# First block of a transformer layer: transposed copies of tiles 0 and 1 in quarters, tiles 2 and 3 transposed by DMA from ScalarE's queue

## The chip, the cores and the metric

The kernel runs on one core of a Trainium2 chip. The metric is the device time of one execution in microseconds; a lower number is better. Five engines work side by side, each through its own instruction stream in order: TensorE (matmul, PE in the profile, with its weight loads as PEld), VectorE (DVE), ScalarE (ACT), GpSimd (POOL) and SyncE (SP), which only issues DMAs here. ScalarE can issue DMAs too; such an instruction stands in its stream among the others.

## The reference

One layer with pre-normalization, on x of 2048 rows and 1024 columns in bfloat16: sliding-window attention with 32 heads and a window of 256, then a dense block with SiLU.

```python
def _layernorm(x, axis=-1, eps=1e-5):
    m = jnp.mean(x, axis=axis, keepdims=True)
    v = jnp.var(x, axis=axis, keepdims=True)
    return (x - m) / jnp.sqrt(v + eps)

def _A_ref(x, wqkv, wo):
    B, S, D = x.shape
    H = 32; Dh = D // H; W = 256
    qkv = (lambda x, *d: x.transpose(*d))((x @ wqkv).reshape(B, S, 3, H, Dh), 2, 0, 3, 1, 4)
    q, k, v = qkv[0], qkv[1], qkv[2]
    scores = jnp.einsum("bhqd,bhkd->bhqk", q, k) * (Dh ** -0.5)
    idx = jnp.arange(S)
    mask = (idx[:, None] - idx[None, :] >= 0) & (idx[:, None] - idx[None, :] < W)
    scores = jnp.where(mask[None, None], scores, -1e9)
    p = _softmax(scores, axis=-1)
    o = jnp.einsum("bhqk,bhkd->bhqd", p, v)
    return (lambda x, *d: x.transpose(*d))(o, 0, 2, 1, 3).reshape(B, S, D) @ wo

def _B_ref(x, w1, w2):
    h = _silu(jnp.einsum("bsd,df->bsf", x, w1))
    return jnp.einsum("bsf,fd->bsd", h, w2)

h = x + _A_ref(_layernorm(x, axis=-1), A_wqkv, A_wo)
h2 = h + _B_ref(_layernorm(h, axis=-1), B_w1, B_w2)
```

## The kernel before

The 2048 rows are worked on in four blocks of 512 rows, and a block in four tiles of 128 rows. The order of the instructions on every engine is written out by hand; waits on semaphores are put in where one engine needs another's result. The change touches the start of block 0 only.

For TensorE the normalized rows must lie transposed, with the 1024 model columns on the partitions in eight pieces of 128 (called kt). `lnT_b[0]` holds them for block 0. For each tile j the way there is: a load of x (`load_x`, L139), statistics on VectorE (`ln_half` L170, then L178), a square root on ScalarE (L206), a reciprocal on VectorE (L209), the normalization on VectorE in two halves of 512 columns (`ln_norm`, L198), and the transpose. The transpose is done in one of two ways. `turn_first` does it on TensorE: four transposes of 128x128 (L217) into one PSUM bank, then one copy of 512 columns by ScalarE into `lnT_b` (L218), for each of two halves. `ln_transpose` does it with one DMA (L202), from SBUF to SBUF, issued from SP's queue. In the kernel before, tiles 0, 1 and 2 of block 0 go through `turn_first`, and tile 3 through `ln_transpose`. The two PSUM banks for the transposes are those that later hold the attention output (`o_ps`, under the name `tp_ps`).

When tile 0 is there, TensorE begins with the V products (`v_group`, L239): for tile j and half c of wv's columns, eight matmuls of 512 columns add up in one of two accumulator banks (`acc`), and ScalarE casts the sum into `v` (L241). The order of the groups (j, c) is (0,0), (1,0), (0,1), (1,1), (2,0), (2,1), (3,0), (3,1). The transposes of tile 1 stand inside the first group, half by half ahead of its matmuls 5 and 7; those of tile 2 stand after the third group. After the V products come the q and k products of the block (`qk_group`, L249), 128 matmuls, and then the attention scores, in the banks `sc`, beside the V, q and k products of block 1.

SP's queue loads in this order: x tile 0, the first half of wv, its second half, x tiles 2 and 3, and the first of four parts of the q/k weights, of 1 MB each (`load_wqkv`, L143). x tile 1 is loaded from ScalarE's queue. Then SP issues tile 3's transpose, and only after it the other three parts of the q/k weights and the x tiles of block 1. Eleven matmuls on zeros (L166) run on TensorE before the first data arrives.

Of the kernel before, what the change touches and what calls it, by code (L numbers as in the profile page):

```python
# [8 lines left out]
BF16 = mybir.dt.bfloat16  # L9
F32 = mybir.dt.float32  # L10
# [4 lines left out]
P = 128  # L15
# [33 lines left out]
def kernel(  # L49
# [10 lines left out]
    nc = tc.nc  # L60
# [3 lines left out]
    S, D = x2d.shape  # L64
# [25 lines left out]
    r_e = big.tile([P, 12288], BF16, name="r_e")  # L90
    r_n = big.tile([P, 1536], BF16, name="r_n")

    ps_sc = tc.tile_pool(name="ps_sc", bufs=1, space=bass.MemoryType.PSUM, reuse_waits="tile")
    sc_pool = ps_sc.__enter__()
    sc = [sc_pool.tile([P, 2, 512], F32, name=f"sc{i}") for i in range(2)]
    o_ps = [ps.tile([P, 8, 64], F32, name=f"o_ps{i}") for i in range(2)]
    tp_ps = [t[:].rearrange("p a b -> p (a b)").bitcast(BF16) for t in o_ps]
    acc_ps = [ps.tile([P, 512], F32, name=f"acc{i}") for i in range(2)]

    def view(region, off, *dims):  # L100
        n = 1
        for d in dims:
            n *= d
        ap = region[:, off:off + n]
        if len(dims) == 2:
            return ap.rearrange("p (a b) -> p a b", b=dims[1])
        if len(dims) == 3:
            return ap.rearrange("p (a b c) -> p a b c", b=dims[1], c=dims[2])
        return ap
# [4 lines left out]
    lnT_b = [view(r_w, 24576, KT, 512), view(r_t, 0, KT, 512)]  # L114
    x_ring = [view(r_o, i * 1024, 1024) for i in range(8)]
# [22 lines left out]
    def load_x(b, j, queue=nc.sync):  # L138
        queue.dma_start(out=x_ring[(b % 2) * 4 + j], in_=x2d[(b * 4 + j) * P:(b * 4 + j + 1) * P, :])  # L139

    def load_wqkv(c0):
        dst = wqk[:, :, c0:c0 + 512] if c0 < 2 * D else wv[:, :, c0 - 2 * D:c0 - 2 * D + 512]
        nc.sync.dma_start(out=dst, in_=wqkv_v[:, :, c0:c0 + 512])  # L143
# [6 lines left out]
    load_x(0, 0)  # L150
    load_wqkv(2 * D)
    load_x(0, 1, nc.scalar)
    load_wqkv(2 * D + 512)
    load_x(0, 2)
    load_x(0, 3)
    load_wqkv(0)

    ident = const.tile([P, P], BF16, name="ident")
    make_identity(nc, ident[:])
    warm = ebuf[0]  # L160
# [2 lines left out]


    for i in range(11):
        nc.tensor.matmul(sc[0][:, i % 2, :], lhsT=warm[:, 0, 0:P], rhs=warm[:, 0, :], start=True, stop=True)  # L166


    def ln_half(xt, stats, c):
        nc.vector.bn_stats(out=stats[:, c, :], in_=xt[:, c * 512:(c + 1) * 512])  # L170

    def ln_stats(xt, st, j, half_done=None):
        stats = half_done
        if stats is None:
            stats = small.tile([P, 2, 6], F32, name="ln_st", tag="ln_st")
            ln_half(xt, stats, 0)
        ln_half(xt, stats, 1)
        nc.vector.bn_aggr(out=st[:, j, :], in_=stats[:])  # L178
# [18 lines left out]
    def ln_norm(xt, st, rs, j):  # L197
        nc.vector.tensor_scalar(out=xt, in0=xt, scalar1=st[:, j, 0:1], scalar2=rs[:, j:j + 1],  # L198
                                op0=ALU.subtract, op1=ALU.mult)

    def ln_transpose(xt, dst, j):
        nc.sync.dma_start_transpose(out=dst[:, :, j * P:(j + 1) * P], in_=xt)  # L202

    def ln_first(xt, st, rs, j, half_done=None, ahead=None):
        ln_stats(xt, st, j, half_done)
        nc.scalar.activation(out=rs[:, j:j + 1], in_=st[:, j, 1:2], func=ACT.Sqrt, bias=eps[:], scale=1.0)  # L206
        if ahead is not None:
            ln_half(ahead[0], ahead[1], 0)
        nc.vector.reciprocal(out=rs[:, j:j + 1], in_=rs[:, j:j + 1])  # L209
        for h in range(2):  # L210
            ln_norm(xt[:, h * 512:(h + 1) * 512], st, rs, j)

    def turn_first(xt, dst, j, halves=(0, 1)):
        for h in halves:
            for i in range(4):
                kt = h * 4 + i
                nc.tensor.transpose(out=tp_ps[h][:, i * P:(i + 1) * P], in_=xt[:, kt * P:(kt + 1) * P], identity=ident[:])  # L217
            nc.scalar.copy(out=dst[:, h * 4:(h + 1) * 4, j * P:(j + 1) * P],  # L218
                           in_=tp_ps[h][:, 0:512].rearrange("p (k q) -> p k q", q=P))

    def ln_tiles(tag):
        st = small.tile([P, 4, 2], F32, name=f"st_{tag}", tag=f"st_{tag}")
        rs = small.tile([P, 4], F32, name=f"rs_{tag}", tag=f"rs_{tag}")
        return st, rs
# [5 lines left out]
    def next_acc():  # L230
        acc_n[0] += 1
        return acc_banks[acc_n[0] % len(acc_banks)]

    def v_group(b, j, c, copy, between=None):
        acc = next_acc()
        for kt in range(KT):
            if between:
                between(kt)
            nc.tensor.matmul(acc, lhsT=lnT_b[b % 2][:, kt, j * P:(j + 1) * P], rhs=wv[:, kt, c * 512:(c + 1) * 512],  # L239
                             start=(kt == 0), stop=(kt == KT - 1))  # L240
        copy(out=v[:, b * 4 + j, c * 16:(c + 1) * 16, 0:DH], in_=acc.rearrange("p (h d) -> p h d", d=DH))  # L241
# [146 lines left out]
    st, rs = ln_tiles("a")  # L388
    half = small.tile([P, 2, 6], F32, name="ln_st", tag="ln_st")
    ln_first(x_ring[0], st, rs, 0, None, (x_ring[1], half))  # L390
    turn_first(x_ring[0], lnT_b[0], 0)
    ln_first(x_ring[1], st, rs, 1, half)

    def turn_1(kt):
        if kt in (5, 7):
            turn_first(x_ring[1], lnT_b[0], 1, (kt // 2 - 2,))

    v_group(0, 0, 0, act, turn_1)
    ln_first(x_ring[2], st, rs, 2)
    v_group(0, 1, 0, act)  # L400
    v_group(0, 0, 1, act)
    turn_first(x_ring[2], lnT_b[0], 2)
    ln_first(x_ring[3], st, rs, 3)
    ln_transpose(x_ring[3], lnT_b[0], 3)
    for c0 in (D, 512, D + 512):
        load_wqkv(c0)
    v_group(0, 1, 1, act)
    v_group(0, 2, 0, act)
    v_group(0, 2, 1, act)
    nc.scalar.activation(out=dummy[:], in_=eps[:], func=ACT.Exp)  # L410
    v_group(0, 3, 0, act)
    v_group(0, 3, 1, act)
    for j in range(4):
        load_x(1, j)

    def ln1_steps(b):
        st, rs = ln_tiles("a")
        xs = [x_ring[(b % 2) * 4 + j] for j in range(4)]
        steps = [lambda j=j: ln_stats(xs[j], st, j) for j in range(4)]
        steps += rstd_steps(st, rs)  # L420
        for j in range(4):
            steps.append(lambda j=j: ln_norm(xs[j], st, rs, j))
        return steps, [lambda j=j: ln_transpose(xs[j], lnT_b[b % 2], j) for j in range(4)]

    def ln2_steps(b):
        st, rs = ln_tiles("b")
        hb = h_blk[b]
        load = lambda: nc.sync.dma_start(out=hb, in_=h_dram[b * 512:(b + 1) * 512, :].rearrange("(j p) d -> p j d", p=P))
        steps = [load]
        steps += [lambda j=j: ln_stats(hb[:, j, :], st, j) for j in range(4)]  # L430
        steps += rstd_steps(st, rs)
        for j in range(4):
            steps.append(lambda j=j: ln_norm(hb[:, j, :], st, rs, j))
        turns = [lambda j=j: ln_transpose(hb[:, j, :], ln2T[b], j) for j in range(4)]
        return steps[:-2] + [turns[0], steps[-2], turns[1], steps[-1]] + turns[2:]
# [22 lines left out]
    def between(kt):  # L458
        k, m = count
        if m * len(first_bursts) >= k * 192:  # L460
            run_late()
            scores_first(k)
            if pending:
                pending.pop(0)()
            for g in range(G):
                if first_where[g, 3, 3][0] == k:
                    pending.extend([lambda g=g: attn_out_first(g, 0), lambda g=g: attn_out_first(g, 1)])
            count[0] += 1
        count[1] += 1
# [102 lines left out]
    for b in range(NB):  # L572
# [4 lines left out]
        for ft in range(FT):  # L577
# [8 lines left out]
            if b == 0 and 6 <= ft < 14:  # L586
                j, c = divmod(ft - 6, 2)
# [60 lines left out]
```

The softmax here doesn't subtract the row's maximum and nothing guards it: scores larger than these inputs give would overflow.

## Time and profile before

| | |
|---|---|
| time, median of 3 runs | 696.99 us (696.95 to 697.09) |
| the profiled execution: time | 696.83 us |
| the profiled execution: span of the instructions | 694.9 us |
| TensorE busy in the span | 684.8 us, 99% |
| first V product starts | 7.42 us |
| first q/k product starts | 22.59 us |
| first score matmul starts | 50.31 us |
| DMA traffic in the span | 60.83 MB, 88 GB/s on average |

The profile is that of one execution. Its page gives the busy time of each engine with its share of the span, the chain of work that ended last, the costliest groups of instructions and the DMA issues. The timeline lists instructions in order of time: start, duration, engine (a "q" behind it marks an instruction of the engine's sequencer, such as a DMA issue), line of the kernel, operation, output<-input by the program's names, and in brackets the idle time ahead of it with what ended it. Several tiles lie in one region: `r_o` holds the x tiles, `r_w` the wqkv weights and `lnT_b[0]`, `r_a` the results q, k and v. The busy time by stretch gives, for a stretch of time, the busy microseconds of PE, PEld, DVE, ACT and POOL, each with its number of instructions, then the granted clock, the DMA share and the rate in GB/s. A matmul of 512 columns is recorded with about 0.38 us, because matmuls overlap; one starts 0.2158 us after another.

### The profile page before, as it was taken

The numbers are of one execution on the slowest core, as the hardware profiler recorded it, in microseconds if no ns is written. First come the engines' busy times: TensorE is split into PE (matmuls) and PEld (weight loads), VectorE is DVE, ScalarE is ACT, GpSimd is POOL, SyncE is SP. The second block draws the span as 40 slices with busy tenths as digits, with TensorE's granted clock in tenths as the row PEclk, the third lists the DMA queues.
The fourth block names the chain that finished last, engine by engine and source line by source line (L and its number), as shares of the span: only waits on it lengthen the run. The fifth ranks groups of instructions, "written<-read, shape, count | busy, mean of one in ns | idle before, by whom it ended". The sixth has DMA issues, their size and how long they took to land.

```text
span 694.9 us, 12233 instructions
## 1 busy us (share of the span) xinstructions
PE 684.8 (99%) x5004; PEld 331.4 (48%) x5091; DVE 288.2 (41%) x608; ACT 257.5 (37%) x322; POOL 174.5 (25%) x391
## 2 busy tenths in 40 slices
PE   8999999999999999999999999999999999999998
PEld 3444454555555555544444444444444444444445
DVE  5257646644443448544316134333133251244111
ACT  4326667777777777621310023300033100233000
POOL 1007667777777677500000000000000000000000
PEclk9999999999999999999999999999999999999999
DMA  7742231036240778880023410023300023100010
GB/s 241 257 63 68 41 99 39 18 66 187 70 129 17 211 253 274 190 311 31 31 75 100 107 38 1 1 87 72 83 1 1 10 96 92 45 1 1 30 39 24
DMA packets 76456, 60.83 MB, mean 88 GB/s; under 512 B 50288, under 2 KB 60528, under 8 KB 76400
## 3 DMA queue, kind: packets, MB, share of 16 engines
q1 hardware_dynamic: 76256, 59.78, 29.6%
q8 instruction: 40, 0.66, 0.4%
q10 hardware_dynamic: 144, 0.26, 0.1%
q14 instruction: 16, 0.13, 0.1%
HBM read 39.85 MB, written 8.39 MB: 69 GB/s over the span
## 4 chain that ended last, share of the span: by engine, by line
PE 98%; issue 1%; DVE 0%; DMA 0%; ACT 0%
PE hacc L558 18%; PE hacc L595 17%; PE acc L249 16%; PE acc L595 10%; PE acc L558 9%; PE acc L239 8%; PE acc L268 7%; PE o_ps L340 4%; PE sc L286 3%; PE hacc L268 1%; PE o_ps L355 1%; PE sc L314 1%; DMA r_o<-in_A_x_dram 0%; DVE ln_st L170 0%; PE o_ps L217 0%
## 5 line engine op out<-in xcount | busy, mean ns | idle before, releaser
L331 POOL TENSOR_SCALAR_AFFINE_SELECT r_e<-r_e 128x256 bf16<-128x256 bf16 (+1 forms) x384 | 171.6, 477 | 116.0 <-ACT r_e L323 64.5
L294 ACT ACTIVATE r_e<-sc 128x1024 bf16<-128x1024 f32 x144 | 139.5, 1021 | 45.1 <-PE sc L286 31.0
L595 PEld LDWEIGHTS <-r_a 128*128 128x128 bf16 x952 | 90.8, 98 | 103.0
L558 PEld LDWEIGHTS <-r_w 128*128 128x128 bf16 x896 | 87.3, 98 | 104.8
L595 PE MATMUL hacc<-r_a 128*128 128x512 bf16 (+2 forms) x607 | 122.0, 360 | 0.5
L558 PE MATMUL hacc<-r_e,r_w 128*128 128x512 bf16 x450 | 100.1, 379 | 0.2
L567 ACT ACTIVATE r_n<-hacc 128x512 f32<-128x512 f32 x30 | 17.9, 597 | 178.9 <-PE hacc L558 175.5
L595 PE MATMUL acc<-r_a 128*128 128x512 bf16 x330 | 73.5, 379 | 0.3
L249 PEld LDWEIGHTS <-r_w 128*128 128x128 bf16 x512 | 46.5, 98 | 57.0 <-issue 7.0
L251 DVE CAST r_a<-acc 128x512 bf16<-128x512 f32 x56 | 38.7, 691 | 72.4 <-PE acc L249 55.8
L249 PE MATMUL acc<-r_t,r_w 128*128 128x512 bf16 x241 | 58.5, 380 | 0.8
L249 PE MATMUL acc<-r_w 128*128 128x512 bf16 x245 | 57.6, 380 | 0.6
L268 PE MATMUL acc<-r_o,r_a 128*128 128x512 bf16 x196 | 48.8, 380 | 0.6
L558 PE MATMUL acc<-r_e,r_w 128*128 128x512 bf16 x207 | 48.4, 379 | 0.6
L340 PEld LDWEIGHTS <-r_e 128*128 128x128 bf16 x1152 | 39.5, 96 | 17.0
L323 ACT ACTIVATE r_e<-sc 128x1024 bf16<-128x1024 f32 x36 | 34.9, 1021 | 21.2 <-PE sc L314 20.1
L340 PE MATMUL o_ps<-r_a,r_e 128*128 128x33 bf16 x1152 | 40.2, 178 | 0.0
L610 DVE SCALAR_TENSOR_TENSOR r_t<-hacc,r_t 128x512 bf16<-128x512 f32 (+2 forms) x22 | 14.0, 635 | 56.7 <-PE hacc L595 56.7
L268 PEld LDWEIGHTS <-r_a 128*128 128x128 bf16 x256 | 23.1, 98 | 29.6 <-issue 5.1
L610 DVE SCALAR_TENSOR_TENSOR r_t<-acc,r_t 128x512 bf16<-128x512 f32 x12 | 8.3, 692 | 64.2 <-PE acc L595 58.8
L568 DVE SCALAR_TENSOR_TENSOR r_a<-r_n,hacc 128x512 bf16<-128x512 f32 x30 | 20.6, 688 | 33.0 <-ACT r_n L567 33.0
L558 PE MATMUL hacc<-r_a,r_w 128*128 128x512 bf16 x138 | 32.4, 379 | 0.3
(71 smaller groups left out, 473.4 us busy)
## 6 DMA issues: line engine op xcount, KB each, us to landing
r_w<-in_B_w_dram SPq DMA_DIRECT2D x8, 896.0 KB, 5.1
r_a<-in_B_w_dram SPq DMA_DIRECT2D x7, 1024.0 KB, 7.8
r_w<-in_A_wqkv_dram SPq DMA_DIRECT2D x6, 1024.0 KB, 8.5
h_dram<-r_t SPq DMA_DIRECT2D x16, 256.0 KB, 2.8
r_t<-h_dram SPq DMA_DIRECT2D x16, 256.0 KB, 2.8
out_dram<-r_t SPq DMA_DIRECT2D x31, 128.0 KB, 1.7
r_o<-in_A_x_dram SPq DMA_DIRECT2D x15, 256.0 KB, 4.1
r_e<-h_dram SPq DMA_DIRECT2D x3, 1024.0 KB, 5.6
```

The source lines that it names most:

```text
L239: nc.tensor.matmul(acc, lhsT=lnT_b[b % 2][:, kt, j * P:(j + 1) * P], rhs=wv[:, kt, c * 512:(c + 1) * 512], start=(kt == 0), stop=(kt == KT ...
L249: nc.tensor.matmul(acc, lhsT=wqk[:, kt, col0:col0 + P], rhs=lnT_b[b % 2][:, kt, :], start=(kt == 0), stop=(kt == KT - 1))
L251: copy(out=(qT, kT)[which][b][:, g, :], in_=acc)
L268: nc.tensor.matmul(acc, lhsT=qT[b][:, g, j * P:(j + 1) * P], rhs=wo[:, g, c * 512:(c + 1) * 512], start=(g == 0), stop=(g == G - 1))
L286: nc.tensor.matmul(sc[hh // 2][:, hh % 2, ch * P:(ch + nq) * P], lhsT=kT[t // 4][r0:r0 + DH, g, (t % 4) * P:(t % 4 + 1) * P], rhs=qT[b][r0 ...
L294: nc.scalar.activation(out=e, in_=sc[pair], func=ACT.Exp, scale=scale)
L323: nc.scalar.activation(out=e, in_=sc[pair], func=ACT.Exp, scale=scale)
L331: nc.gpsimd.affine_select(out=ap, in_=ap, pattern=[[0, 2], [0, n], [sgn, P]], compare_op=ALU.is_ge if upper else ALU.is_gt, fill=0.0, base ...
L340: nc.tensor.matmul(o_ps[pair][:, qt * 2 + hh, 0:VW], lhsT=e_of(i, kind, pair)[:, hh, ch * P:(ch + 1) * P], rhs=v[:, b * 4 + kt, g * 4 + pa ...
L558: nc.tensor.matmul(acc, lhsT=w1[:, kt, ft * P:(ft + 1) * P], rhs=ln2T[b][:, kt, :], start=(kt == 0), stop=(kt == KT - 1))
L595: nc.tensor.matmul(acc[:, 0:c1 - c0], lhsT=gT[:, ft, j * P:(j + 1) * P], rhs=w2[ft // 4][:, ft % 4, c0:c1], start=(ft == 0), stop=(ft == F ...
L610: nc.vector.scalar_tensor_tensor(out=t_out[j % 2][:, c0:c1], in0=acc[:, 0:c1 - c0], scalar=0.5, in1=t_in[j % 2][:, c0:c1], op0=ALU.mult, o ...
```

## The change

Tiles 0 and 1 of block 0 are normalized in four quarters of 256 columns. `turn_first` goes by quarters too: two transposes into a bank of their own, then a copy of 256 columns. Four new PSUM banks (`tp`) serve for this; the score banks `sc`, which held these places, are allocated when the V products of block 0 have been written out, and the eleven matmuls on zeros write into `o_ps`. All transposes of tile 1 stand ahead of the last matmul of the first V group. The normalization in quarters holds for tiles 2 and 3 as well, since they use the same `ln_first`. Tiles 2 and 3 are transposed by DMA, issued from ScalarE's queue: tile 2 after the cast of the second group, tile 3 after the cast of the fourth. x tile 2 is loaded ahead of the second half of wv. The four parts of the q/k weights follow x tile 3 on SP's queue without a transpose between them.

```diff
--- before.py
+++ after.py
@@ -90,11 +90,10 @@
     r_e = big.tile([P, 12288], BF16, name="r_e")
     r_n = big.tile([P, 1536], BF16, name="r_n")
 
-    ps_sc = tc.tile_pool(name="ps_sc", bufs=1, space=bass.MemoryType.PSUM, reuse_waits="tile")
-    sc_pool = ps_sc.__enter__()
-    sc = [sc_pool.tile([P, 2, 512], F32, name=f"sc{i}") for i in range(2)]
+    ps_tp = tc.tile_pool(name="ps_tp", bufs=1, space=bass.MemoryType.PSUM, reuse_waits="tile")
+    tp_pool = ps_tp.__enter__()
+    tp_ps = [tp_pool.tile([P, 1024], BF16, name=f"tp{i}") for i in range(4)]
     o_ps = [ps.tile([P, 8, 64], F32, name=f"o_ps{i}") for i in range(2)]
-    tp_ps = [t[:].rearrange("p a b -> p (a b)").bitcast(BF16) for t in o_ps]
     acc_ps = [ps.tile([P, 512], F32, name=f"acc{i}") for i in range(2)]
 
     def view(region, off, *dims):
@@ -150,10 +149,11 @@
     load_x(0, 0)
     load_wqkv(2 * D)
     load_x(0, 1, nc.scalar)
+    load_x(0, 2)
     load_wqkv(2 * D + 512)
-    load_x(0, 2)
     load_x(0, 3)
-    load_wqkv(0)
+    for c0 in (0, D, 512, D + 512):
+        load_wqkv(c0)
 
     ident = const.tile([P, P], BF16, name="ident")
     make_identity(nc, ident[:])
@@ -163,7 +163,7 @@
 
 
     for i in range(11):
-        nc.tensor.matmul(sc[0][:, i % 2, :], lhsT=warm[:, 0, 0:P], rhs=warm[:, 0, :], start=True, stop=True)
+        nc.tensor.matmul(o_ps[i % 2][:].rearrange("p a b -> p (a b)"), lhsT=warm[:, 0, 0:P], rhs=warm[:, 0, :], start=True, stop=True)
 
 
     def ln_half(xt, stats, c):
@@ -198,8 +198,8 @@
         nc.vector.tensor_scalar(out=xt, in0=xt, scalar1=st[:, j, 0:1], scalar2=rs[:, j:j + 1],
                                 op0=ALU.subtract, op1=ALU.mult)
 
-    def ln_transpose(xt, dst, j):
-        nc.sync.dma_start_transpose(out=dst[:, :, j * P:(j + 1) * P], in_=xt)
+    def ln_transpose(xt, dst, j, queue=nc.sync):
+        queue.dma_start_transpose(out=dst[:, :, j * P:(j + 1) * P], in_=xt)
 
     def ln_first(xt, st, rs, j, half_done=None, ahead=None):
         ln_stats(xt, st, j, half_done)
@@ -207,16 +207,16 @@
         if ahead is not None:
             ln_half(ahead[0], ahead[1], 0)
         nc.vector.reciprocal(out=rs[:, j:j + 1], in_=rs[:, j:j + 1])
-        for h in range(2):
-            ln_norm(xt[:, h * 512:(h + 1) * 512], st, rs, j)
-
-    def turn_first(xt, dst, j, halves=(0, 1)):
-        for h in halves:
-            for i in range(4):
-                kt = h * 4 + i
+        for h in range(4):
+            ln_norm(xt[:, h * 256:(h + 1) * 256], st, rs, j)
+
+    def turn_first(xt, dst, j):
+        for h in range(4):
+            for i in range(2):
+                kt = h * 2 + i
                 nc.tensor.transpose(out=tp_ps[h][:, i * P:(i + 1) * P], in_=xt[:, kt * P:(kt + 1) * P], identity=ident[:])
-            nc.scalar.copy(out=dst[:, h * 4:(h + 1) * 4, j * P:(j + 1) * P],
-                           in_=tp_ps[h][:, 0:512].rearrange("p (k q) -> p k q", q=P))
+            nc.scalar.copy(out=dst[:, h * 2:(h + 1) * 2, j * P:(j + 1) * P],
+                           in_=tp_ps[h][:, 0:256].rearrange("p (k q) -> p k q", q=P))
 
     def ln_tiles(tag):
         st = small.tile([P, 4, 2], F32, name=f"st_{tag}", tag=f"st_{tag}")
@@ -392,24 +392,28 @@
     ln_first(x_ring[1], st, rs, 1, half)
 
     def turn_1(kt):
-        if kt in (5, 7):
-            turn_first(x_ring[1], lnT_b[0], 1, (kt // 2 - 2,))
+        if kt == 7:
+            turn_first(x_ring[1], lnT_b[0], 1)
 
     v_group(0, 0, 0, act, turn_1)
     ln_first(x_ring[2], st, rs, 2)
     v_group(0, 1, 0, act)
+    ln_transpose(x_ring[2], lnT_b[0], 2, nc.scalar)
     v_group(0, 0, 1, act)
-    turn_first(x_ring[2], lnT_b[0], 2)
     ln_first(x_ring[3], st, rs, 3)
-    ln_transpose(x_ring[3], lnT_b[0], 3)
-    for c0 in (D, 512, D + 512):
-        load_wqkv(c0)
     v_group(0, 1, 1, act)
+    ln_transpose(x_ring[3], lnT_b[0], 3, nc.scalar)
     v_group(0, 2, 0, act)
     v_group(0, 2, 1, act)
     nc.scalar.activation(out=dummy[:], in_=eps[:], func=ACT.Exp)
     v_group(0, 3, 0, act)
     v_group(0, 3, 1, act)
+
+    ps_tp.__exit__(None, None, None)
+    ps_sc = tc.tile_pool(name="ps_sc", bufs=1, space=bass.MemoryType.PSUM, reuse_waits="tile")
+    sc_pool = ps_sc.__enter__()
+    sc = [sc_pool.tile([P, 2, 512], F32, name=f"sc{i}") for i in range(2)]
+
     for j in range(4):
         load_x(1, j)
```

## The prediction

> **What bounds the kernel now.** The page comes first: TensorE is busy for 99% of the span, and the chain that ended last is 98% PE.
>
> ```profile
> PE 684.8 (99%) x5004; PEld 331.4 (48%) x5091; DVE 288.2 (41%) x608; ACT 257.5 (37%) x322; POOL 174.5 (25%) x391
> PE 98%; issue 1%; DVE 0%; DMA 0%; ACT 0%
> ```
>
> So only two things move the end: work added to or taken from TensorE, and idle time opened or closed on it. The change touches the first 23 us, so next I read the timeline there. The V products of block 0 (L239) run from 7.42 to 22.59 us, where the first q/k product (L249) starts. One 512-column matmul follows another by 0.2158 us, a 128-column transpose by 0.0556 us. 64 matmuls and 16 transposes (tiles 1 and 2) make 13.81 + 0.89 = 14.70 us of the 15.17; what is left is two waits and crumbs.
>
> ```profile
> 5.87 0.74 DVE L198 TENSOR_SCALAR r_o<-r_o,st_a,rs_a 128x512 bf16<-128x512 bf16 x2
> 8.28 0.74 DVE L198 TENSOR_SCALAR r_o<-r_o,st_a,rs_a 128x512 bf16<-128x512 bf16 x2
> 8.75 0.40 PE L217 MATMUL o_ps<-ident,r_o 128*128 128x128 bf16 x4
> 13.30 0.61 PE L217 MATMUL o_ps<-ident,r_o 128*128 128x128 bf16 x8
> 16.25 1.34 SPq L202 DMA_TRANSPOSE r_w<-r_o  x1
> 19.12 0.76 PEld L239 LDWEIGHTS <-r_w 128*128 128x128 bf16 x5 [0.52 <-DMA r_w<-r_o]
> ```
>
> The second line feeds the third: TensorE has run five V matmuls, is through with them at 8.51 and idles 0.24 us until tile 1 is normalized. The last two lines are tile 3's DMA transpose: issued at 16.25, landed 2.83 us later (median to landing of L202 in that stretch: 2.8), and TensorE stands 0.20 us for it (the weight load's 0.52 includes time in which matmuls still ran). It was issued into an idle DMA system, as busy times by stretch show (the last two columns are DMA share and GB/s):
>
> ```profile
> 8.00:11.00 3.00, 2.92 (x21) 1.39 (x19) 1.32 (x4) 1.70 (x4) 0.00 (x0) 1.00 1.07 395
> 13.90:17.50 3.60, 3.60 (x19) 1.63 (x17) 1.81 (x6) 2.04 (x6) 0.00 (x0) 1.00 0.00 0
> 19.20:30.00 10.80, 10.75 (x50) 4.90 (x52) 0.99 (x2) 4.24 (x7) 0.00 (x0) 1.00 1.03 366
> ```
>
> SP's in-order queue holds the last three q/k weight loads behind that transpose. The changed kernel releases them at once.
>
> [...] The trace has one meeting of two queues, x tile 0 and wv on SP (q1) and x tile 1 on ScalarE (q10). DMA in 2.85 to 3.50 us, then in 3.50 to 4.10:
>
> ```profile
> q10 hardware_dynamic: 82, 0.17, 79.3%
> q1 hardware_dynamic: 43, 0.06, 25.9%
> q10 hardware_dynamic: 61, 0.09, 48.4%
> q1 hardware_dynamic: 85, 0.09, 42.7%
> ```
>
> In the single packet records, tile 1 starts only as tile 0 runs out, and the wv load, whose issue ended at 1.67, only as tile 1 runs out. They took turns by whole transfers, not one descriptor each[...].[...]
>
> **The change, part by part.**
>
> *Quarters for tiles 0 and 1.* A VectorE normalization of 1024 columns takes 0.540 us, of 512 0.411; successive ones start 0.457 and 0.328 apart. Continuing both: 256 columns take 0.345, 0.263 apart. Four quarters occupy VectorE for 1.05 us until its next instruction, two halves 0.65: +0.40 per tile. Tile 0: quarters ready at 6.22, 6.48, 6.74, 7.01 (halves: 6.29, 6.61). The last two transposes issue at 7.07 and 7.13, so the first V matmul starts at 7.18 instead of 7.42, a gain of 0.24; the quarter copies (two copies of 512 start 0.48 apart and take 0.59; an estimate from these is 0.37 us, 0.26 apart) are ready in time. Tile 1 pays: its second half of statistics starts 0.40 late, and its square root, held before by ScalarE's copies until 7.74, is now held by VectorE until 7.90. Normalization starts at 8.44 instead of 8.28; its last quarter is ready at 9.58. All eight transposes now stand ahead of the last matmul of the first group, which starts at 9.74 (before: 9.63). The next group starts at 9.96 instead of 9.85: **+0.11**, the early start is lost again. Four PSUM banks rather than two remove no wait: the bank's next writer comes over 1.5 us after its copy. The score banks are allocated after these copies, used first at 50.3 us: nothing.
>
> *Tile 2's transposes leave TensorE and ScalarE.* 8 x 0.0556 = **-0.44**, and two 0.59 us copies leave ScalarE, which nobody waited for.
>
> *x tile 2 second.* It lands at about 7.8 (wv's first half landed at 7.17, and 256 KB add 0.65) instead of 10.56. The second wv half slips from 9.92 to 10.56 and is first read at 11.69: hidden by 1.1 us. VectorE reaches tile 2 at 9.49 instead of 10.58; its normalization ends at 9.49 + 2.10 (statistics 1.32, aggregate 0.21, root and reciprocal 0.57) + 1.13 = 12.72.
>
> With nothing else, the remaining seven groups of 1.726 us would end at 9.96 + 12.09 = 22.05: 0.54 us under the 22.59. That is the most the change can bring, 0.08%.
>
> *Tiles 2 and 3 by DMA on ScalarE's queue.* ScalarE issues tile 2 at 12.75 (waiting for VectorE; the cast ahead of it ends at 12.47). Issue holds ScalarE for 1.34 us, until 14.09; behind it is queued the cast of the third group, complete at 13.6, whose bank the fifth group needs at 15.14. The cast runs 14.1 to 14.7: hidden, unless the issue takes a further 0.45 us. Tile 3's root is also behind it: 14.58, normalized by 16.25, issued 16.28, on ScalarE until 17.62. Landing with an idle DMA system: 12.75 + 2.83 = 15.58 and 19.11. The fifth group is due at 15.14, so tile 2 is late by 0.44 even then; tile 3 gives 19.15 for the seventh group, as before (19.13). Sum: 0.0.
>
> *The q/k loads move up.* They no longer wait behind a transpose; the semaphores that the last two wait for belong to loads landed by about 8 us. A 1 MB load takes 2.69 us in a row (tile x3 landed at 11.19, the first q/k load at 13.88). So D is moving until 16.57, the third until 19.26, the fourth until 21.95: exactly while both transposes need the DMA engines. The loads' earlier landing is worth nothing, TensorE did not wait for them. What the transposes lose is what the before trace doesn't show. From below: nothing lost, +0.0. From above: first come, first served, tile 2 moves after 21.7.
>
> I take turns by whole transfers, which the two queues showed. A transpose has 1024 packets of 256 bytes at 17.5 ns over 16 engines: 1.12 us. Tile 2's packets are ready at 14.09 behind D, move from 16.3 to 17.4, land at 17.8 (0.4 as before); the fifth group starts at 17.85, 2.7 us late. Tile 3 is ready at 17.62 behind the third load, moves from 20.1, lands at 21.6. Seventh group at max(17.85 + 3.45, 21.65) = 21.65, V ends at 25.10: **+2.5 us**. TensorE idles 2.7 us at once[...].
>
> **Rivals.**
>
> *Not slower: fair sharing or small packets.* The transposes take half of the engines' time, so each loses 1.12 us: landings 16.70 and 20.23, seventh group at 20.28, V ends at 23.73, +1.1 us; with no loss +0.0, at best -0.5. [...] Against it: q10 and q1 above did not mix. It decides when tile 3's landing comes in under 20.5 us: 696.5 to 698.3.
>
> *First come, first served over both queues.* For it: wv waited for tile 1. Tile 2 lands at 23.1, tile 3 at 24.2; the fifth group starts at 23.15, V ends at 30.05: +7.5 us[...]: 704.5 to 706.2.
>
> *One descriptor each in turn.* 64 packets per engine at 17.5 + 46 ns are 4.06 us, 2.94 more: landings 18.5 and 22.6, +3.5 us, 700.5. The meeting above speaks against it.
>
> **How the numbers follow.** The profiled execution took 696.83 (span 694.9, 1.9 around it), 0.16 under the median of 696.99; the differences are added to the median. Whole transfers in turn 0.38: 699.5. One each 0.08: 700.5. First come 0.15: 704.5 to 706.2. Light sharing 0.36: 696.5 to 698.3. A surprise below, 0.03. A measurement can tell 0.2%, 1.4 us, from no change. The light case lies within it but for a sliver; faster by 1.4 us has no source I can find: 0.03. Slower 0.61, same 0.36. As the signs are split, the likeliest case's own range is 698.6 to 700.6. The range for 8 in 10 runs from 696.5 to 705.5.
>
> **What would show it.** L202 moves to the ScalarE queue, with landings of 5 us instead of 2.8; TensorE's wait for DMA r_w<-r_o grows to some 3 us in total; first V matmul near 7.2, second group near 9.96, first L249 near 25.1. If L249 starts before 23.9, sharing was light; after 29, first come, first served. If L239 waits for ScalarE's casts of acc instead, the issue held that engine. DMA share in 14 to 20 us should be near 1.

## The result and the profile after

The changed kernel takes 704.56 us (median of 5 runs, 703.96 to 704.88) against 696.99 (5 runs, 696.94 to 697.42): 7.57 us slower, ratio 1.0106 with a 95% interval of 1.0091 to 1.0121. The forecast was slower, at 699.5 with a range of 696.5 to 705.5. The direction came and the measured time lies inside the range, near its upper end. The likeliest case, whole transfers in turn, forecast a third of the loss that came, and its own range of 698.6 to 700.6 missed.

The profiled execution of the changed kernel took 704.8 us, 7.97 more than that of the kernel before. First the page: busy times, and the chain that ended last by engine.

```profile
PE 687.8 (98%) x4996; PEld 331.8 (47%) x5083; DVE 289.5 (41%) x616; ACT 256.9 (37%) x324; POOL 174.5 (25%) x391
PE 96%; DMA 2%; DVE 1%; issue 1%; ACT 0%
```

DMA has come into the chain with 2%. The page also shows that TensorE is busy 3.0 us longer, although eight transposes were taken from it: some of its work ran slower. The timeline says where (columns as before):

```profile
5.79 1.11 DVE L198 TENSOR_SCALAR r_o<-r_o,st_a,rs_a 128x256 bf16<-128x256 bf16 x4
7.24 1.67 PE L239 MATMUL acc<-r_w 128*128 128x512 bf16 x7
8.75 1.03 PE L217 MATMUL tp<-ident,r_o 128*128 128x128 bf16 x8
12.58 1.33 ACTq L202 DMA_TRANSPOSE r_w<-r_o  x1
16.11 1.56 ACTq L202 DMA_TRANSPOSE r_w<-r_o  x1
21.17 9.63 PE L239 MATMUL acc<-r_w 128*128 128x512 bf16 x32 [6.00 <-DMA r_w<-r_o]
30.63 0.59 PE L249 MATMUL acc<-r_w 128*128 128x512 bf16 x2
```

Up to 15 us nothing is lost: the second V group starts at 9.83 (before: 9.85), and TensorE is ready for the fifth group at 15.01. Then it stands until tile 2's transpose lands at 21.12, 8.54 us after its issue. The last 32 V matmuls, which take 6.91 us at 0.2158 each, take 9.46 from start to start of the next stage. The first q/k product comes at 30.63 instead of 22.59, 8.04 us late, and the first score matmul at 58.35 instead of 50.31, 8.04 late too: between the two nothing is made up and nothing more is lost.

What the DMA engines did meanwhile, by the DMA view of two stretches, 14 to 16.5 us and then 17 to 20:

```profile
q1 hardware_dynamic: 958, 0.96, 108.7%
q1 hardware_dynamic: 859, 0.86, 81.3%
q10 hardware_dynamic: 858, 0.22, 32.3%
```

Columns: packets, MB, share of the 16 engines. Tile 2's issue ended at 13.91, but its queue, q10, has no packet in the first stretch; its first comes at 16.70. Until then SP's queue (q1) goes on alone: the second q/k load lands at 16.69, and 267 packets of the third have moved as well (4363 packets of 1 KB up to 16.69, of which wv and the first two q/k loads make 4096). Then the queues take turns by one packet: 859 against 858, and in most of the single records a load packet starts 14 ns after a transpose packet and the next transpose packet 42 to 43 ns after that. A transpose packet is 256 bytes and a load packet 1 KB, so the transpose gets 0.22 MB while the loads get 0.86. By the durations of the packets (medians of the records: 18 and 46 ns), 64 of each on every engine come to 64 x (17.5 + 46) ns = 4.06 us, an estimate, instead of 1.12; from tile 2's first packet to its last, at 20.68, it is 3.98. The busy times of the same span (columns PE, PEld, DVE, ACT, POOL, clock, DMA share, GB/s):

```profile
13.90:16.50 2.60, 1.27 (x6) 0.39 (x4) 1.37 (x6) 1.37 (x3) 0.00 (x0) 1.00 1.09 386
21.10:26.20 5.10, 5.03 (x12) 1.79 (x13) 0.00 (x0) 0.59 (x1) 0.00 (x0) 0.50 1.04 357
26.60:30.60 4.00, 4.00 (x20) 1.79 (x19) 0.00 (x0) 2.55 (x4) 0.00 (x0) 1.00 0.02 4
```

In the second row TensorE's granted clock is 0.50: twelve matmuls in 5.10 us, one every 0.427. That costs 12 x 0.211 = 2.5 us more.

The sum: wait for tile 2, 21.17 - 15.01 = +6.16 (the 6.00 of the timeline counts from the recorded end of the last matmul, which overlaps the next); lowered clock +2.55; against that tile 2's transposes on TensorE (-0.44), tile 3's wait (-0.20) and small gaps (-0.03). Together +8.04.

### The profile page after: what moved, and what is told of

It reads as the page before. It is cut to its first block, busy times and chain, and to the rows that moved or that the text cites. A ratio compares the mean times of both kernels' runs of the same rounds, so it can differ in the third digit from the quotient of the medians.

```text
span 703.1 us, 12226 instructions
## 1 busy us (share of the span) xinstructions
PE 687.8 (98%) x4996; PEld 331.8 (47%) x5083; DVE 289.5 (41%) x616; ACT 256.9 (37%) x324; POOL 174.5 (25%) x391
## 4 chain that ended last, share of the span: by engine, by line
PE 96%; DMA 2%; DVE 1%; issue 1%; ACT 0%
PE hacc L562 18%; PE hacc L599 17%; PE acc L249 16%; PE acc L599 10%; PE acc L562 9%; PE acc L239 7%; PE acc L268 7%; PE o_ps L340 4%; PE sc L286 3%; PE hacc L268 1%; PE o_ps L355 1%; DMA r_w<-r_o 1%; PE sc L314 1%; DVE ln_st L170 1%; DVE r_o L198 0%
## 5 line engine op out<-in xcount | busy, mean ns | idle before, releaser
L249 PE MATMUL acc<-r_w 128*128 128x512 bf16 x245 | 57.6, 380 | 0.6
L239 PE MATMUL acc<-r_w 128*128 128x512 bf16 x123 | 31.8, 405 | 6.3 <-DMA r_w<-r_o 6.0
```

Of the source, the lines that this page charges most:

```text
L249: nc.tensor.matmul(acc, lhsT=wqk[:, kt, col0:col0 + P], rhs=lnT_b[b % 2][:, kt, :], start=(kt == 0), stop=(kt == KT - 1))
```

## The experiments

The theory: the q/k loads, released early, share the DMA engines with the transposes and delay tile 2, and the idling that follows lowers TensorE's clock. The rivals: ScalarE's queue is slow for transposes; DMA transposes of two tiles are slow from any queue; the quarters or the order of the loads cost time; the late matmuls are slow for another reason than idling. Each experiment is an edit of the changed kernel, but for the one on quarters, which edits the kernel before. Line numbers shift by one or two between kernels. The start varies by almost 1 us between profiles with the landing of x tile 0 (3.47 to 4.43), so moments are compared from there where that matters.

**The loads held back, transposes on ScalarE's queue.**

```diff
-    for c0 in (0, D, 512, D + 512):
-        load_wqkv(c0)
+    load_wqkv(0)
...
     ln_transpose(x_ring[3], lnT_b[0], 3, nc.scalar)
+    gate = const.tile([P, 16], BF16, name="gate")
+    nc.sync.dma_start(out=gate[:], in_=lnT_b[0][:, 0, 3 * P:3 * P + 16])
+    for c0 in (D, 512, D + 512):
+        load_wqkv(c0)
```

> Tiles 2 and 3 stay on ScalarE's queue; the last three q/k loads are issued only after a 4 KB copy on SP that waits for tile 3's transpose to land. Theory (the q/k loads take the DMA engines from the transposes): landings back to 2.8 us each, tile 2 at about 15.4 and tile 3 at 18.9, [...]first q/k product at 22.4, 696.8 us (696.4 to 697.3). Rival (a transpose issued from ScalarE's queue is slow in itself): landings stay near 8.5 us, first q/k product near 30.6, 704.6 us. Rival (quarters and the order of the x loads cost): 700 us or more with landings of 2.8.

Measured: 698.89 us, ratio 1.0023 (1.0014 to 1.0033). Landings 3.1 us each, first q/k product at 23.12 (19.12 after x tile 0's landing; before: 18.93), clock 1.0 throughout. So ScalarE's queue isn't slow in itself, and 5.9 of the 7.6 us are gone when the loads are held back. The expected 696.8 did not come, and VectorE's timeline shows why:

```profile
30.23 0.69 DVE L250 CAST r_a<-acc 128x512 bf16<-128x512 f32 x1 [2.69 <-PE acc L248]
34.57 1.29 DVE L169 BATCH_NORM_STATS2 ln_st<-r_o 128x6 f32<-128x512 bf16 x2 [3.64 <-DMA r_o<-in_A_x_dram]
36.02 0.63 DVE L250 CAST r_a<-acc 128x512 bf16<-128x512 f32 x1
```

The gate also delays block 1's x tiles, which stand behind the loads. VectorE waits 3.64 us for the first of them, x tile 4, with a cast of `acc` queued behind that wait, and TensorE, whose next `acc` waits 1.3 us for that cast, idles 1.6 us from 35.1. The next experiment tests this reading.

**The same gate, block 1's x tiles ahead of the last two loads.** In place of the loop after the gate, and of the later loop that loads these tiles:

```diff
+    load_wqkv(D)
+    for j in range(4):
+        load_x(1, j)
+    load_wqkv(512)
+    load_wqkv(D + 512)
```

> The gated run on ScalarE's queue (the last three q/k loads after tile 3's landing) with block 1's x tiles loaded right behind the second q/k load, ahead of the third and fourth. In the gated run VectorE stood 3.6 us in its order for x tile 4, landed at 34.5, with a cast of acc behind it, and TensorE idled 1.6 us at 35. Theory (that wait is all that is left of the loss): x tile 4 lands near 29, the idle time at 35 is gone, 697.2 us (696.8 to 697.6). Rival (TensorE idles at 35 for another reason, such as its instructions coming late): 698.9 us as before.

Measured: 697.39 us, ratio 1.0001 (0.9993 to 1.0010); the idle time at 35 is gone. With the loads out of the way, what is left of the change makes no difference to the time.

**Both transposes on SP's queue, the loads behind them.** Both calls of `ln_transpose` lose `nc.scalar`, and the last three loads follow the second call.

> Both transposes go through SP's queue and the last three q/k loads stand behind them, all else as in the changed kernel. Theory (loads against transposes): as the gated run on ScalarE's queue, a little earlier since ScalarE's square root for tile 3 no longer stands behind a transpose issue: tile 3 lands near 18.5, first q/k product at 22.35, 696.75 us. Rival (transposes of two tiles by DMA are slow wherever they are issued): tile 2 lands after 18 us, 699 us or more.

Measured: 697.14 us, ratio 1.0000 (0.9992 to 1.0009), landings 2.81 and 2.73 us after issue, first q/k product at 22.74, which is 18.75 after x tile 0's landing, 0.18 sooner than in the kernel before. The theory holds; two tiles by DMA are not slow in themselves.

**Both on SP's queue, the loads ahead.** Only `nc.scalar` is dropped from the two calls.

> The changed kernel with both transposes on SP's queue, where they stand behind all four q/k loads. One queue keeps its order: tile 2's packets come after the fourth load, which without transposes beside it ends near 22; tile 2 lands near 23.3, tile 3 near 24.5, the fifth group starts near 23.3 after 8 us of idling, the lowered clock costs 2.5 us, the first q/k product comes near 32.7, 707 us (705.5 to 708.5). So ScalarE's queue, though its transposes were late, saved some 2 us against this. Rival (the second queue saved nothing, the transposes in the changed kernel came as late as they would in one queue): tile 2 lands near 21.1, 704.6 us.

Measured in 2 runs: 706.81 us, ratio 1.0138 (1.0117 to 1.0158). SP's timeline, and TensorE's:

```profile
14.30 8.07 SPq L202 DMA_TRANSPOSE r_w<-r_o  x2
23.62 8.46 PE L239 MATMUL acc<-r_w 128*128 128x512 bf16 x32 [7.83 <-DMA r_w<-r_o]
```

Tile 2 lands at 23.57, as first come, first served says. The issue of the first transpose alone holds SP for 5.65 us, against 1.33 with the loads behind it; that the queue was full is my reading, no view shows it. The last 32 matmuls took 8.29 us from start to start instead of the expected 9.4: only the first seven ran at the lowered clock of 0.50, which so cost 1.38 us instead of 2.55. Against the kernel before the loss is 9.5 us, to 7.6 with ScalarE's queue: some 2 us, from two runs. In the profiled executions, counted from x tile 0's landing, tile 2 lands 1.83 us sooner through ScalarE's queue, but the first q/k product comes only 0.66 sooner, since more of the lowered clock falls on matmuls there. So the second queue did more here than save issue time: it let the transposes pass part of the loads, which was worth between 0.7 and 2 us.

**Only quarters, on the kernel before.** The order of the loads stays, and so does the way of tiles 2 and 3 (TensorE and SP's DMA); tile 2's transposes on TensorE go by quarters as well. The main lines of the edit:

```diff
+        n = 4 if j < 2 else 2
-        for h in range(2):
-            ln_norm(xt[:, h * 512:(h + 1) * 512], st, rs, j)
+        for h in range(n):
+            ln_norm(xt[:, h * D // n:(h + 1) * D // n], st, rs, j)
...
-        if kt in (5, 7):
-            turn_first(x_ring[1], lnT_b[0], 1, (kt // 2 - 2,))
+        if kt == 7:
+            turn_first(x_ring[1], lnT_b[0], 1)
```

> The kernel before with only the quarters and the four banks (normalization in quarters for tiles 0 and 1, turn_first in quarters for tiles 0 to 2, all transposes of tile 1 ahead of matmul 7); loads and tile 3's transpose as before. Theory (the early start is given back at tile 1): first V product at 7.24 instead of 7.42, second group within 0.1 us of 9.85, first q/k product within 0.2 of 22.6, no difference in time: 697.0. Rival (quarters are a gain or a loss of their own): second group earlier or later by 0.3 us or more, and the first q/k product with it.

Measured: 697.27 us, ratio 1.0002 (0.9993 to 1.0011). From x tile 0's landing, the first V product starts at 3.50 us (before 3.75) and the second group at 6.24 (before 6.19). The 0.25 won at tile 0 is given back at tile 1, as worked out.

**TensorE kept busy through the wait.**

```diff
+    for i in range(28):
+        nc.tensor.matmul(o_ps[i % 2][:].rearrange("p a b -> p (a b)"), lhsT=warm[:, 0, 0:P], rhs=warm[:, 0, :], start=True, stop=True)
     v_group(0, 2, 0, act)
```

> The changed kernel with 28 extra matmuls on zeros (6.04 us) ahead of the fifth V group, in the time in which TensorE waited for tile 2. Their results are not used. Theory (the 12 matmuls at 0.427 us after the wait are the lowered clock after idling): the fifth group starts at 21.1 to 21.2 as before and runs at 0.216 us a matmul; 2.5 us come back, of which about 1.0 goes to waiting for tile 3, which lands at 25.7: first q/k product near 29.2, 703.1 us. Rival (the matmuls are slow because the DMA engines write SBUF beside them): spacing stays 0.427 until the loads end at about 26 us, 704.6 us.

Measured: 705.54 us, ratio 1.0121 (1.0106 to 1.0136). Busy times by stretch, and DMA from 21 to 23 us:

```profile
21.30:24.70 3.40, 3.40 (x17) 1.47 (x16) 0.00 (x0) 0.59 (x1) 0.00 (x0) 1.00 1.17 222
24.70:27.10 2.40, 0.22 (x2) 0.00 (x0) 0.00 (x0) 2.07 (x3) 0.00 (x0) 1.00 1.08 384
DMA packets 407, 0.28 MB, mean 138 GB/s; under 512 B 204, under 2 KB 406, under 8 KB 406
q8 instruction: 1, 0.02, 3.2%
```

The clock stays at 1.00 and the group runs at 0.216 us a matmul. The DMA engines moved less than in the changed kernel, though (222 GB/s in the first row, against 357 above), so the next run has to settle whether it was their traffic. The expected time missed. Tile 3 landed at 27.09 instead of 25.66, and the 2.5 us went into waiting for it (second row: TensorE busy 0.22 of 2.40 us). One packet of 16 KB on queue q8, an instruction fetch, came at 21.25 (in the changed kernel at 29.0) and lasted 1.0 us; from 21.8 to 23.0 both data queues all but stood still, hence the 138 GB/s. I had left the extra instructions' own fetch out.

**The same with fewer instructions.** Seven float32 matmuls on zeros instead of the 28.

> As the kept-busy run, but with 7 matmuls of 512 columns in float32 on zeros instead of 28 in bfloat16; results not used. In the kept-busy run an instruction fetch of 16 KB came 8 us earlier, met tile 3's transpose and held it by 1.5 us, which ate what the clock gave back. Seven instructions move the fetch less. Theory (idling lowers the clock): the fifth group runs at 0.216 us a matmul from its start near 21.2, tile 3 lands near 25.7, the seventh group starts there, first q/k product near 29.2, 703.1 us. If the fetch again meets tile 3, the first q/k product comes near 30.6. Rival (slow matmuls come from something else than idling): 0.427 us a matmul for some 5 us after the start, 704.6.

Measured: 705.08 us, ratio 1.0111 (1.0096 to 1.0127). First this run, then the changed kernel, in the stretch after tile 2's landing:

```profile
21.40:24.80 3.40, 3.40 (x17) 1.46 (x16) 0.00 (x0) 0.59 (x1) 0.00 (x0) 1.00 1.12 381
20.50:24.80 4.30, 3.63 (x9) 1.34 (x10) 0.00 (x0) 0.00 (x0) 0.00 (x0) 0.50 1.12 369
```

The DMA share is the same 1.12, the clock 1.00 against 0.50: idling, not DMA traffic, had lowered it. Again tile 3 is late: landing 10.97 us after issue, at 27.46, with the fetch at 25.25 among its last packets. The alternative that I had named came. So the lowered clock is shown, but a gain of time from keeping it up is not: even at the 25.66 of the changed kernel tile 3 would have taken back about 1.0 of the 2.5 us, and its later landing took the rest. That the fetch is what held tile 3 is argued from its moment in these two runs; in the kernel before, a fetch of the same size at 23.11 met the loads alone and the rate from 22.5 to 25 us stayed at 379 GB/s.

**How the two queues take turns.** Two runs of this. In the first, each q/k load is cut in four:

```diff
     for c0 in (0, D, 512, D + 512):
-        load_wqkv(c0)
+        for k0 in range(0, KT, 2):
+            nc.sync.dma_start(out=wqk[:, k0:k0 + 2, c0:c0 + 512], in_=wqkv_v[:, k0:k0 + 2, c0:c0 + 512])
```

> The changed kernel with each 1 MB q/k load cut into four transfers of 256 KB (1 KB rows as before). In the changed kernel tile 2's packets were due at 13.9 us and began only at 16.7, when the running 1 MB load had ended. Theory W (a transfer whose turn has begun is finished first): the first packets come within 0.7 us of the end of the issue, then one packet each in turn for 4.1 us; tile 2 lands 6.5 us after its issue instead of 8.5, at about 19.1, and the kernel takes about 702 us. Theory P[...]: first packets still 2.5 to 3 us late, landing 8.5 us, 704.5 us. Theory G[...]: also late, by one small load's time or more.

In the second, the gate stands ahead of the last two loads only, so two run early:

```diff
-    for c0 in (0, D, 512, D + 512):
-        load_wqkv(c0)
+    load_wqkv(0)
+    load_wqkv(D)
```

> The changed kernel with only the first two q/k loads ahead; the other two wait on SP for tile 3's transpose to land. So one 1 MB load (until about 16.6 us) runs beside tile 2, and SP has nothing waiting for room. Theories W and P (what has been taken in goes first): no transpose packets from 14.0 to about 16.3, then tile 2 alone in 1.1 us; landing 5.3 to 5.5 us after its issue. Theory G (only a load that waits for room holds up the other queue): packets of both queues in turn from 14.0, about 140 of each in 0.5 us, landing 5.5 to 5.8 us. In both cases the fifth group starts near 18.1, the first q/k product near 25.0, and the time is near 699.5 us, since half of the load traffic is gone from beside the transposes.

Measured in 2 runs each: with the loads cut 703.29 us, ratio 1.0088 (1.0070 to 1.0107), tile 2 landing 6.80 us after its issue; with two loads early 700.86 us, ratio 1.0053 (1.0035 to 1.0072), landing after 6.13 us, later than either theory had it. DMA with two loads early, 14 to 16.5 us and 17 to 19:

```profile
q1 hardware_dynamic: 856, 0.87, 109.5%
q10 hardware_dynamic: 1996, 0.50, 126.5%
q1 hardware_dynamic: 11, 0.01, 1.2%
```

The first transpose packet moves at 16.81, 2.97 us after the end of its issue, as the running load ends, although the next load on SP was held back until tile 3's transpose had landed: theory G, by which a load waiting on SP holds up the other queue, falls. With the loads cut, from 14.8 us (the end of tile 2's issue) to 16.6, and from 17 to 18.5:

```profile
q1 hardware_dynamic: 722, 0.69, 109.3%
q10 hardware_dynamic: 938, 0.24, 99.6%
q1 hardware_dynamic: 118, 0.11, 32.1%
```

Here, too, the transpose waits 2.0 us, through 722 packets, which is more than two transfers of 256 packets: theory W, one transfer finished first, falls. What fits all three kernels is theory P in outline: some 45 to 66 packets of SP's queue per engine went ahead of the first transpose packet (722 over 16 engines here, 1067 in the changed kernel from 13.91 to 16.70), whatever transfers they belonged to. That the engines had already taken these packets in is my reading; no view shows it. With the loads held back, in the first experiment, tile 2's first packet came at 14.27, right at the end of its issue. The landing of 6.80 us is near W's number and not P's 8.5 all the same, for another reason: after the delay the transpose had the engines nearly to itself, 938 packets to 118. In my reading of this kernel's program, which no view shows, SP's later loads wait for the transposes to land. But three small loads issued before 16.3 did not take turns with tile 2 either, and why not stays open.

**A version meant to beat both.** SP's queue with the loads behind, quarters for tiles 0 and 1 alone, halves for tiles 2 and 3.

> A version meant to beat both: quarters for tiles 0 and 1 only, tiles 2 and 3 normalized in halves (0.4 us less VectorE time each) and transposed through SP's queue, the last three q/k loads behind them. Theory: tile 2 is issued near 12.1 and lands near 15.0, when the fifth group is due; tile 3 lands before 18.3, no wait; the V products end 0.5 to 0.7 us earlier than in the kernel before, counted from x tile 0's landing: 696.5 us, ratio 0.999 to 1.000. Rival (VectorE's waits for block 1's x tiles or the start decide): 697.0, no difference.

Measured: 696.89 us, ratio 0.9996 (0.9988 to 1.0004). The first q/k product comes 18.39 us after x tile 0's landing (before: 18.93), 0.54 sooner as expected, but the time can't tell a gain of 0.08% from none. No version is shown to beat the kernel before.

## Why the prediction was right, and where its size was off

- **TensorE is the bound, and the first 23 us decide: right.** The shift of the first q/k product, 8.04 us, is the shift of the first score matmul.
- **The quarters come to nothing: right.** First V product at 7.24 (forecast 7.18), second group at 9.83 (9.96); alone, 1.0002.
- **At most 0.54 us to gain: not contradicted.** With the loads behind the transposes on SP the changed kernel gained 0.18 in the trace; the version with halves, which differs from it, gained 0.54. Neither shows in the time.
- **Issue holding ScalarE: right.** 1.33 us; the casts behind it delayed nobody.
- **The transposes collide with the q/k loads: right**, shown by holding the loads back (1.0001 with the x tiles in time, 1.0000 on SP).
- **"I take turns by whole transfers, which the two queues showed": the term that was mis-sized.** The moment of its first half came: tile 2's packets waited until 16.7 (forecast 16.3). The reason did not hold even there: packets of the third load had moved ahead of them, and with the loads cut the wait went across transfers. Then "move from 16.3 to 17.4" failed: tile 2 moved not alone but one packet for one of the loads, in 4.0 us instead of 1.1, and landed at 21.12 instead of 17.8. The rival with 0.08, one each in turn, was half of the truth, with the initial wait missing in it. The two x tiles of the before trace have eight packets per engine each, too few to tell turns of whole transfers from packets that were ahead already.
- **"TensorE idles 2.7 us at once": fell with it.** It idled 6.0 us, and the lowered clock, which the likeliest case does not price, cost 2.5 us. From the forecast of 25.10: +3.32 for tile 2, -0.35 for tile 3's wait that no longer showed, +2.55 for the clock, 30.62.
- **First come, first served** gave the right time, +7.5, by the wrong way, which is luck: in the changed kernel the transposes moved beside the third and fourth loads. The sign named for it, a first q/k product after 29, came too and would have misled. That the range reached up to 705.5 was owed to this rival; the part of it above 704.5, up to 706.2, was my estimate, and no trace of the kernel before shows it. In the run with one queue, where tile 2 landed behind the loads, at 23.57, the loss was 9.5.
- **Light sharing, at 0.36, did not come.** Its 1.1 us or less were my estimate; no trace of the kernel before showed such sharing.

On the clock: an idle time of 3.6 us (two loads early) left it at full speed in the profiled execution (mean granted clock 1.0; 0.998 in the other one); 4.3 (loads cut), 6.0 (the changed kernel) and 7.8 us (one queue) came with a lowered clock, the mean 0.995 in each profiled execution. The length of the idling alone does not decide: with the loads cut, the clock fell 3.1 us after the idling began. In these three profiled executions it stayed at 0.50 for 6.8 us, from 19.5 to 26.4 in the changed kernel; the means of the other executions of the three kernels, 0.993 to 0.998, leave open whether it is always as long. Only what fell on matmuls cost time: 5.7, 5.2 and 2.8 us from TensorE's restart to the full clock.

## What to carry to other kernels

Before a load is moved earlier, ask which short transfer on the critical path it will then meet. Here a transfer on a second queue still waited 2 to 3 us behind the loads, and after that, in the changed kernel, each of its packets of 256 bytes got one turn for one of 1 KB (859 to 858). Price a wait of TensorE with the clock that follows it (here 2.5 us of loss after a wait of 6.0), and look whether the next transfer is due right behind, before counting on winning either back. A load held back is not free either (here 1.5 us, 698.89 to 697.39): check what stands behind it in its queue, and whose casts stand behind that wait.

## What the runs showed of the hardware that was not expected

- In the changed kernel packets of the two queues alternated one for one: 859 of 1 KB to 858 of 256 bytes over 3 us. A transpose of 256 KB stretched from 1.1 to 4.0 us.
- Ahead of that, a newly issued transfer waited 2.0 us (loads cut) to 3.0 us (two loads early) while some 45 to 66 packets per engine of the other queue went first; with the loads held back the first packet came at 14.27, right at the end of the issue.
- The lowered clock of 0.50 lasted 6.8 us in each of the three profiled executions that had it, whether TensorE worked again after 1.2 us of it or only after 4.0.
- Twice a transpose in flight landed some 1.4 us late when an instruction fetch of 16 KB, about 1 us long, came beside it; 28 more matmuls had brought the fetch 7.75 us forward. That the fetch was the cause is not shown.
- The issue of a DMA transpose behind four loads of 1 MB on the same queue held SP for 5.65 us instead of 1.33.
